# Gated linear attention before a maxout layer: sums kept in PSUM on VectorE, and all queues in a new order

## The chip, the cores and the metric

One core of one Trainium2 chip. The time is that of the device for one execution, in microseconds (us). The kernel before took 141.57 us (median of 3 runs, 141.08 to 141.87). The engines are named as in the profile: PE (TensorE), DVE (VectorE), ACT (ScalarE), POOL (GpSimd) and SP (SyncE, which here issues DMAs).

## The reference, cut to what matters

```python
batch, n_heads, seq, head_dim = (4, 8, 768, 48)      # q, k, v, f_logit, float32
f = 1.0 / (1.0 + np.exp(-f_logit))
for t in range(S):
    state = f[:, :, t, :, None] * state + np.einsum('bhd,bhe->bhde', k[:, :, t], v[:, :, t])
    y[:, :, t] = np.einsum('bhd,bhde->bhe', q[:, :, t], state)
x = y.transpose(0, 2, 1, 3).reshape(3072, 384)
out = np.maximum(x @ w1, x @ w2) @ w_out             # w1, w2: 384 x 1024, w_out: 1024 x 384
```

A linear attention whose 48 x 48 state decays by a gate of its own in each row, and behind it a layer with the greater of two products.

## The kernel before, in words

The 768 positions of each of the 4 batches are cut into 3 windows of 256, so there are 12 units of work, numbered s = 4 * window + batch (0 to 11). A partition holds an even position and the odd one behind it; the upper and the lower 64 partitions are the two halves of a window, h = 0 and 1, with one update of the state each. Within a half the positions meet through a masked product (A, m), over the halves through the state.

The greater of two products is computed as relu(x (w1 - w2)) w_out + x (w2 w_out). So the weights need work of their own at the start: the difference `wd` (in four quarters), w_out cast, w2 transposed, and the product `m2` of w2 and w_out.

Everything is cut into steps, and the text `ORDER` lists them. Each engine works through its own steps in that order, and waits where an operand is not ready or a buffer is not free. A word of it is a step's letters, its unit (and part), its engine where there is a choice (v = DVE, a = ACT, p = POOL, s = SP), and behind @ the PSUM bank that it uses (0 to 7), or for a load the slot in SBUF. Texts below name steps in this way, mostly without the bank: `Q5p` is step Q of unit 5 on POOL. The steps, with the line that the profile shows:

- loads on SP: `Lf Lk Lq Lv` (inputs, L114), `Wa Wb` (halves of w1 and w2, L125), `Wo` (halves of w_out, L129); stores `O` (L439) and `P` (parts of the last unit, L433)
- ACT: `E` (L191), `F` (L195), `G` (L199) make the gate's logarithm and its exponentials from f; `X` (`inv`, L216) and `Z` (`dec`, L221) are exponentials of the sums that `C` left in PSUM
- DVE or POOL: `e` (L202) adds the logarithms of a pair; `i` (L225) and `K` (L236) scale k; `j` (L229, DVE) and `Q` (L239) scale q; `V` (L103) casts v. Their inputs lie in SBUF
- PE: `C` (L206, L209) cumulative sums; `t`, `u` (L256) transpose K's and Q's results into a pair of banks; `A` (L273) products of q and k, two parts; `S` (L313) starts the output with the state's part, `y` (L341) finishes it; `D` (L357) sums k and v for the new state
- out of PSUM: `U` (L103, `trs`) copies t's and u's result; `m` (L281, DVE) masks A's; `z` (L329, DVE) reads one column, so that `y` comes behind `S`; `Y` (L103, `xT`) copies the output of `y`
- the state, part h: `n` (L373, DVE) adds D's sum and the state before, `N` (L378, DVE or POOL) multiplies by the decay in `dec`; where there is no state before, `n` (L375) multiplies the sum by the decay at once, and no N follows
- the layer: PE `d` (L396, four parts of a unit, 6 matmuls each) multiplies by `wd`, `r` (L405 on ACT, L407 on DVE) applies relu to two parts, PE `o` (L417 with `m2`, 3 matmuls; L420, 8 matmuls) gives the output, `b` (L103, `ob`) copies it
- weights: `wc` casts w2 (L103), PE `wt` (L456) transposes it, `wx` copies that out of PSUM, `wo` casts w_out, PE `wm` (L472) forms `m2`, `wn` copies it, `ws` (L482) forms a quarter of `wd`

The result of `n` lies in SBUF (`tmp_s`, float32, three buffers), whoever does the N behind it. The bank of `D` can be written again when `n` has read it.

Of the kernel before, what the change touches and what calls it, by code (L numbers as in the profile page):

```python
# [17 lines left out]


ORDER = """  # L20
Lf0s@12 Lk0s@13 Lq0s@14 Lv0s@15 E0 Lf1s@16 F0 Lk1s@17 e0v G0 i0v C0@0 Lq1s@12 Z0 X0 K0v V0a Lv1s@18
j0v D0@0 Q0v t0@2 Wb0s E1 n0.0v u0@2 n0.1v F1 Wa0s U0v@2 N0.1p Wb1s G1 Wa1s e1v A0.0@2 Wo0s i1p C1@0
Wo1s m0.0v@2 A0.1@4 X1 S0@6 Z1 K1p m0.1v@4 Lf2s@16 V1a z0 y0 j1v t1@4 Q1v Y0a@6 wc0a u1@4 D1@0 U1v@4
wc1a wt0@6 ws0p n1.0v A1.0@4 A1.1@2 n1.1v m1.0v@4 S1@0 wt1@7 ws1p Lf3s@12 wx0v@6 d0.0@4 z1 wx1a@7
m1.1v@2 wc3p d0.1@5 wc2a wt3@7 ws2v y1 r0.0a@4 wt2@6 ws3v Y1a@0 d0.2@4 Lq2s@0 wo1p wx2v@6 d1.2@0
wx3a@7 d1.0@2 wo0p Lk2s@2 d1.1@3 wo3a wo2p d0.3@5 r1.0v@2 Lv2s@10 wm0@7 E2 r0.1v@4 F2 Lq3s@16 wm2@6
E3 e2p wn0v@7 wm1@4 Lk3s@11 F3 j2v wn2a@6 e3p C2@7 wn1v@4 d1.3@1 Lv3s@12 G2 X2 i2v o0.0@6 Z2 K2v
Lf5s@8 V2a Q2v t2@4 r1.1a@0 D2@2 Lf4s@10 u2@4 n2.0v C3@7 j3v G3 o1.0@0 Lq4s@0 N1.1p X3 U2v@4 b0.0a@6
i3p Z3 n2.1v A2.0@4 Lk4s@2 K3p S2@6 A2.1@2 m2.0v@4 o0.1@1 V3a b1.0a@0 Lv4s@12 m2.1v@2 Q3p E5 D3@4 z2
t3@2 F5 Lk5s@11 b0.1v@1 y2 n3.0v N2.1p E4 u3@2 n3.1v e5p o1.1@1 Y2v@6 Lv5s@16 F4 U3v@2 G4 e4p  # L30
Lq5s@10 d2.0@6 b1.1a@1 j4v C4@0 A3.0@2 i4p X4 A3.1@4 Lf7s@8 d2.1@7 m3.0v@2 Z4 K4p G5 d2.2@0 r2.0a@6
Lf8s@9 m3.1v@4 S3@2 d2.3@1 V4a Q4p C5@6 z3 r2.1v@0 y3 Lq7s@3 X5 t4@4 Y3a@2 D4@0 O0s u4@4 n4.0v Z5
d3.0@2 Lq6s@0 i5v U4a@4 d3.2@6 j5v Lf6s@12 d3.1@3 K5v d3.3@7 r3.0a@2 N4.0p Lk7s@11 o2.0@4 Q5p n4.1v
E7 r3.1v@6 F7 t5@2 V5v A4.0@6 Lk6s@10 A4.1@0 b2.0a@4 e7p u5@2 m4.0v@6 o2.1@5 U5a@2 N3.1p Lv6s@16
m4.1v@0 C7@4 S4@6 b2.1a@5 j7v A5.0@0 Lv7s@8 D5@2 X7 N4.1p z4 o3.0@5 n5.0v Z7 N5.0v E6 Q7p Lq8s@2
n5.1v m5.0v@0 E8 S5@2 y4 b3.0a@5 Lv10s@9 j6v A5.1@0 F6 o3.1@5 m5.1v@0 Y4a@6 e6p O2s Lf9s@3 z5 G6
d4.0@6 G7 b3.1v@5 i6p O1s C6@4 d4.2@0 X6 i7v y5 Z6 K6v Lq11s@12 d4.1@7 Y5a@2 K7v Lk8s@10 d4.3@1
r4.0a@6 Q6v d5.0@2 Lf11s@11 t6@4 r4.1a@0 N5.1p t7@6 u6@4 V7p u7@6 d5.1@3 U6v@4 F8 d5.2@0 r5.0a@2
U7v@6 D7@4 Lf10s@8 d5.3@1 V6a o4.0@2 n7.0v r5.1a@0 N7.0p Lk9s@0 e8v G8 j8v A7.0@6 Lq9s@16 D6@0 n7.1v
C8@3 n6.0v o4.1@4 Z8 m7.0v@6 N6.0p Lq10s@6 X8 Q8p b4.0a@2 n6.1v A7.1@6 b4.1a@4 S7@0 O3s A6.0@2  # L40
m7.1v@6 o5.0@5 E9 Lv8s@7 i8p F9 z7 Lk10s@3 m6.0v@2 G9 e9p y7 V10a Lv9s@2 A6.1@2 N7.1p S6@6 o5.1@4
b5.0a@5 m6.1v@2 E10 z6 F10 Y7v@0 C9@2 O4s y6 X9 Lk11s@8 j9v b5.1a@4 d7.0@0 K8v Z9 O5s d7.2@4 E11 Q9p
Y6v@6 d7.1@1 F11 Lv11s@11 d6.0@6 r7.0a@0 d7.3@5 i9v d6.1@7 K9v r7.1a@4 d6.2@2 V8v t9@0 r6.0a@6 e11v
t8@4 u9@0 u8@4 d6.3@3 U9v@0 U8a@4 o7.0@6 r6.1v@2 A8.1@4 j11v b7.0a@6 A9.0@0 A8.0@2 V9p D8@7 G10
o7.1@6 m8.0v@2 G11 i11p n8.0v m8.1v@4 o6.1@7 N8.0p b7.1a@6 i10p O7s m9.0v@0 N6.1p C11@4 D9@5 X11
A9.1@0 S8@2 n9.0v o6.0@6 Z11 z8 N9.0p m9.1v@0 Q11p S9@0 y8 z9 e10v y9 b6.0v@6 Y8a@2 C10@4 b6.1v@7
Y9a@0 d8.0@2 K11v O6s d8.2@6 Z10 X10 d9.0@0 K10v d9.2@4 d9.1@1 j10v d8.1@3 Q10p r9.0a@0 d9.3@5
r8.0v@2 d8.3@7 r9.1a@4 t10@0 r8.1v@6 t11@2 u10@0 u11@2 o9.0@4 U10a@0 U11v@2 V11v A11.0@2 b9.0a@4
A10.0@0 A11.1@6 m11.0v@2 D11@5 o8.1@4 m11.1v@6 o8.0@2 n11.0v m10.0v@0 N11.0p S11@6 b8.0a@2 D10@5
A10.1@0 z11 n10.0v y11 N10.0v m10.1v@0 S10@2 o9.1@5 Y11a@6 b8.1a@4 z10 y10 b9.1v@5 O9s d11.0@4  # L50
Y10v@2 O8s d11.2@0 d11.1@5 d11.3@1 r11.0a@4 d10.0@2 d10.2@6 r11.1v@0 d10.1@3 d10.3@7 r10.0a@2
o11.0@0 r10.1a@6 o10.0@1 b11.0v@0 P11.0s o10.1@0 b10.0v@1 o11.1@6 b10.1v@0 O10s o11.2@7 b11.1v@6
P11.1s b11.2a@7 P11.2s
"""


# [1 line left out]
def kernel(  # L58
# [311 lines left out]
    def step_n(s, h):  # L370
        if has_state(s, h):
            tmps[s, h] = work.tile([C, NP, D], F32, name="tmp_s", tag="tmp_s", bufs=3)
            nc.vector.tensor_add(tmps[s, h], sadd[s][h][:, :, 0:D], state_before(s, h)[:, 1::2, :])  # L373
        else:
            nc.vector.tensor_mul(state_of(s)[:, h, 1::2, :], sadd[s][h][:, :, 0:D], decay(s, h))  # L375

# [167 lines left out]
```

## Time and profile before

The profile shows one execution. Its first line gives the span, from the first instruction to the last.

| | |
|---|---|
| time of the profiled execution | 141.12 us |
| its span | 139.3 us |
| median of 3 runs | 141.57 us |
| instructions in the span | 5772 |
| mean granted clock of PE | 1.000 |
| DMA: bytes and mean rate over the span | 28.68 MB, 206 GB/s |

The engines' lines of the page give busy us, the share of the span, and behind x the instructions. The line of digits gives the busy share in tenths in 40 equal slices of the span, 3.48 us each. A group of instructions shows the engine, the operation, output <- inputs, their sizes, the count, then busy us, the mean ns of one, and behind a bar the idle time just before them with what ended it. A row of the timeline begins with its start and duration in us. A row of the waits gives the total us, how many times, and the longest.

### The profile page before, as it was taken

The numbers are of one execution on the slowest core, as the hardware profiler recorded it, in microseconds if no ns is written. First come the engines' busy times: TensorE is split into PE (matmuls) and PEld (weight loads), VectorE is DVE, ScalarE is ACT, GpSimd is POOL, SyncE is SP. The second block draws the span as 40 slices with busy tenths as digits, with TensorE's granted clock in tenths as the row PEclk, the third lists the DMA queues.
The fourth block names the chain that finished last, engine by engine and source line by source line (L and its number), as shares of the span: only waits on it lengthen the run. The fifth ranks groups of instructions, "written<-read, shape, count | busy, mean of one in ns | idle before, by whom it ended". The sixth has DMA issues, their size and how long they took to land.

```text
span 139.3 us, 5772 instructions
## 1 busy us (share of the span) xinstructions
PE 122.4 (88%) x2575; PEld 91.6 (66%) x2575; DVE 99.6 (72%) x155; ACT 83.1 (60%) x119; POOL 56.6 (41%) x64
## 2 busy tenths in 40 slices
PE   0026699999899999996999999999999999999991
PEld 0024677876567788665688657886678876778670
DVE  5778968756988787789778686967957689643130
ACT  3646464769677679796578687978126470404400
POOL 7604519526188795736601382530860501000000
PEclk9999999999999999999999999999999999999999
DMA  4999999999999999999999999891113000032014
GB/s 112 271 261 264 374 386 378 334 257 238 274 266 239 256 268 274 273 263 253 292 316 273 244 260 292 239 319 50 59 59 118 0 5 7 5 132 98 3 53 169
DMA packets 54617, 28.68 MB, mean 206 GB/s; under 512 B 50240, under 2 KB 51648, under 8 KB 54592
## 3 DMA queue, kind: packets, MB, share of 16 engines
q1 hardware_dynamic: 54592, 28.32, 76.7%
q8 instruction: 20, 0.33, 1.0%
q14 instruction: 5, 0.04, 0.1%
HBM read 23.59 MB, written 4.72 MB: 203 GB/s over the span
## 4 chain that ended last, share of the span: by engine, by line
PE 79%; DMA 9%; DVE 3%; POOL 3%; SPq 2%; ACT 2%; issue 1%; DVEq 0%; POOLq 0%
PE banks L396 23%; PE banks L420 21%; PE banks L417 9%; DMA slots<-in_moe_w_dram 6%; PE banks L341 5%; PE banks L256 4%; PE banks L273 4%; PE banks L313 4%; PE banks L472 3%; DMA slots<-in_f_logit_dram 3%; POOL wd L482 3%; PE banks L357 2%; PE banks L206 2%; DVE st L378 1%; SPq L114 1%; SPq L125 1%
## 5 line engine op out<-in xcount | busy, mean ns | idle before, releaser
L420 PE MATMUL banks<-wo,gT 128*128 128x384 bf16 (+2 forms) x200 | 35.3, 320 | 0.0
L396 PE MATMUL banks<-xT,wd 128*128 128x256 bf16 x288 | 34.6, 274 | 0.3 <-POOL wd L482 0.3
L281 DVE TENSOR_TENSOR at_m<-banks,mask 128x1024 bf16<-128x1024 f32 x24 | 28.7, 1218 | 6.0 <-PE banks L273 6.0
L396 PEld LDWEIGHTS <-wd 128*128 128x128 bf16 x288 | 27.3, 98 | 4.5 <-POOL wd L482 0.6
L420 PEld LDWEIGHTS <-gT 128*128 128x128 bf16 x200 | 19.3, 98 | 12.0
L405 ACT ACTIVATE gT<-banks 128x1024 bf16<-128x1024 f32 x16 | 16.0, 1022 | 9.5 <-PE banks L396 9.2
L239 POOL TENSOR_TENSOR qp<-slots,dec 128x768 bf16<-128x768 f32 x8 | 15.1, 1888 | 11.4 <-ACT dec L221 6.0
L103 ACT COPY ob<-banks 128x384 f32<-128x384 f32 (+2 forms) x18 | 9.0, 501 | 16.8 <-PE banks L420 14.1
L378 POOL TENSOR_TENSOR st<-tmp_s,dec 128x192 bf16<-128x192 f32 x14 | 7.9, 566 | 23.6 <-DVE tmp_s L373 21.4
L417 PE MATMUL banks<-m,xT 128*128 128x384 bf16 (+2 forms) x75 | 16.1, 321 | 0.4 <-DVE m L103 0.4
L407 DVE TENSOR_SCALAR gT<-banks 128x1024 bf16<-128x1024 f32 x8 | 9.7, 1222 | 5.7 <-PE banks L396 5.3
L191 ACT ACTIVATE gate<-slots 128x768 f32<-128x768 f32 x12 | 10.0, 845 | 4.6 <-DMA slots<-in_f_logit_dram 4.6
L103 DVE COPY ob<-banks 128x384 f32<-128x384 f32 (+2 forms) x11 | 5.9, 542 | 8.5 <-PE banks L420 8.1
L103 DVE COPY trs<-banks 128x2048 bf16<-128x2048 bf16 x8 | 9.7, 1220 | 3.0 <-PE banks L256 3.0
L341 PE MATMUL banks<-at_m,vb 64*64 64x128 bf16 x576 | 11.7, 224 | 0.0
L103 ACT CAST xT<-banks 128x768 bf16<-128x768 f32 x8 | 6.4, 798 | 8.8 <-PE banks L341 8.7
L225 POOL TENSOR_TENSOR slots<-slots,one 128x384 f32<-128x384 f32 x7 | 7.6, 1084 | 9.8 <-ACT one L199 6.4
L273 PE MATMUL banks<-trs 48*64 48x128 bf16 x384 | 9.6, 234 | 1.3 <-DVE trs L103 1.3
L313 PE MATMUL banks<-trs,st 48*64 48x128 bf16 x240 | 8.7, 227 | 2.2 <-DVE look L329 1.1
L195 ACT ACTIVATE ell<-gate 128x768 f32<-128x768 f32 x12 | 10.1, 843 | 0.6
L236 DVE TENSOR_TENSOR kp<-slots,inv 128x768 bf16<-128x768 f32 x9 | 8.6, 963 | 2.6 <-issue 1.4
L206 PE MATMUL banks<-e,u_inc 128*128 128x384 bf16 x12 | 4.3, 356 | 6.8 <-DVE e L202 6.8
(64 smaller groups left out, 180.1 us busy)
## 6 DMA issues: line engine op xcount, KB each, us to landing
slots<-in_f_logit_dram SPq DMA_DIRECT2D x12, 384.0 KB, 6.3
slots<-in_k_dram SPq DMA_DIRECT2D x12, 384.0 KB, 6.4
slots<-in_q_dram SPq DMA_DIRECT2D x12, 384.0 KB, 6.2
slots<-in_v_dram SPq DMA_DIRECT2D x12, 384.0 KB, 6.1
out_dram<-ob SPq DMA_DIRECT2D x11, 384.0 KB, 5.4
slots<-in_moe_w_dram SPq DMA_DIRECT2D x4, 768.0 KB, 9.1
...
```

Source lines behind the costliest of these rows:

```text
L103: (nc.scalar.copy if e == "a" else engines[e].tensor_copy)(out, in_)
L191: nc.scalar.activation(flat(gate[s]), flat(loaded[s]["f"]), AF.Exp, bias=0.0, scale=-1.0)
L195: nc.scalar.activation(flat(ell[s]), flat(gate[s]), AF.Ln, bias=1.0, scale=1.0)
L239: engines[e].tensor_mul(pad("qp", s)[:, :, :, 0:D], by_parity(loaded[s]["q"]), both(dec[s][:, 0:HD].rearrange("p (h d) -> p h d", h=H)))
L273: nc.tensor.matmul(out=ps[h * HC:(h + 1) * HC, j % 2, par, :], lhsT=t[rows, h, 0, j, par, :], rhs=t[rows, h, 1, j].rearrange("p a t -> p ( ...
L281: nc.vector.tensor_mul(at[s][:, jj].rearrange("p r j a t -> p (r j) (a t)"), banks[:, b:b + 2, :].rearrange("p r (j x) -> p (r j) x", j=2) ...
L313: nc.tensor.matmul(out=ys[s][h][cols, kt, :], lhsT=window(state_before(s, h)[rows], head // 2, off), rhs=tr[s][rows, h, 1, head // 2].rear ...
L341: nc.tensor.matmul(out=ys[s][h][cols, kt, :], lhsT=window(vb[rows, par], head, off), rhs=m[rows, head // 4, head % 2, head // 2 % 2, par, ...
L396: nc.tensor.matmul(out=ps[:, f, :], lhsT=wd[:, kt, ff * C:(ff + 1) * C], rhs=x_flat(g)[:, kt, :], start=(kt == 0), stop=(kt == KT - 1))
L405: nc.scalar.activation(dst, src, AF.Relu)
L417: nc.tensor.matmul(out=ps, lhsT=x_flat(g)[:, kt, cols], rhs=m2[:, kt, m], start=(kt == 0), stop=False)
L420: nc.tensor.matmul(out=ps, lhsT=gT[g][:, ff, cols], rhs=wo[:, ff, m], start=False, stop=(ff == FG - 1))
```

## The change

A sum whose N is done by DVE stays where D left it: `n` adds the state before to it in its PSUM bank, and N reads it there. For the other N nothing changes but the order.

```diff
+    words = ORDER.split()
...
     def step_n(s, h):
         if has_state(s, h):
-            tmps[s, h] = work.tile([C, NP, D], F32, name="tmp_s", tag="tmp_s", bufs=3)
-            nc.vector.tensor_add(tmps[s, h], sadd[s][h][:, :, 0:D], state_before(s, h)[:, 1::2, :])
+            sums = sadd[s][h][:, :, 0:D]
+            tmps[s, h] = sums if f"N{s}.{h}v" in words else work.tile([C, NP, D], F32, name="tmp_s", tag="tmp_s", bufs=3)
+            nc.vector.tensor_add(tmps[s, h], sums, state_before(s, h)[:, 1::2, :])
```

The order is new as a whole: the same 540 steps, with other places, banks and slots, and for some another engine. It was made with GpSimd and VectorE holding each other up as their steps come. The steps with a choice of engine go, before and after, to:

| step | before | after |
|---|---|---|
| e | 5 DVE, 7 POOL | 1 DVE, 11 POOL |
| i | 5 DVE, 7 POOL | 4 DVE, 8 POOL |
| K | 9 DVE, 3 POOL | 8 DVE, 4 POOL |
| Q | 4 DVE, 8 POOL | 6 DVE, 6 POOL |
| V | 7 ACT, 3 DVE, 2 POOL | 5 ACT, 2 DVE, 5 POOL |
| N | 2 DVE, 14 POOL | 6 DVE, 10 POOL |
| r | 16 ACT, 8 DVE | 20 ACT, 4 DVE |
| b | 16 ACT, 9 DVE | 18 ACT, 7 DVE |
| wc | 3 ACT, 1 POOL | 2 ACT, 1 POOL, 1 DVE |
| wn | 2 DVE, 1 ACT | 3 DVE |
| wo | 3 POOL, 1 ACT | 2 POOL, 2 ACT |
| U, Y, ws, wx | | the same numbers |
| P | 3 SP | 2 SP, 1 ACT |

The start of the order, up to the first `o`:

```
before:
Lf0s@12 Lk0s@13 Lq0s@14 Lv0s@15 E0 Lf1s@16 F0 Lk1s@17 e0v G0 i0v C0@0 Lq1s@12 Z0 X0 K0v V0a Lv1s@18
j0v D0@0 Q0v t0@2 Wb0s E1 n0.0v u0@2 n0.1v F1 Wa0s U0v@2 N0.1p Wb1s G1 Wa1s e1v A0.0@2 Wo0s i1p C1@0
Wo1s m0.0v@2 A0.1@4 X1 S0@6 Z1 K1p m0.1v@4 Lf2s@16 V1a z0 y0 j1v t1@4 Q1v Y0a@6 wc0a u1@4 D1@0 U1v@4
wc1a wt0@6 ws0p n1.0v A1.0@4 A1.1@2 n1.1v m1.0v@4 S1@0 wt1@7 ws1p Lf3s@12 wx0v@6 d0.0@4 z1 wx1a@7
m1.1v@2 wc3p d0.1@5 wc2a wt3@7 ws2v y1 r0.0a@4 wt2@6 ws3v Y1a@0 d0.2@4 Lq2s@0 wo1p wx2v@6 d1.2@0
wx3a@7 d1.0@2 wo0p Lk2s@2 d1.1@3 wo3a wo2p d0.3@5 r1.0v@2 Lv2s@10 wm0@7 E2 r0.1v@4 F2 Lq3s@16 wm2@6
E3 e2p wn0v@7 wm1@4 Lk3s@11 F3 j2v wn2a@6 e3p C2@7 wn1v@4 d1.3@1 Lv3s@12 G2 X2 i2v o0.0@6 Z2 K2v
...
after:
Lf0s@12 Lk0s@13 Lq0s@14 Lv0s@15 E0 Lf1s@16 F0 Lk1s@12 G0 e0p i0v C0@0 Lq1s@17 j0v X0 Z0 K0v Lv1s@18
V0a Q0p D0@0 Wb0s t0@2 n0.0v E1 n0.1v u0@2 F1 Wa0s U0v@2 Wb1s G1 e1p Wa1s N0.1v S0@2 Wo0s A0.0@0 i1p
Wo1s z0 C1@4 m0.0v@0 A0.1@6 X1 Z1 Lf2s@16 K1p j1v V1a Q1v m0.1v@6 t1@4 wc0a u1@4 D1@0 U1a@4 y0 n1.0v
n1.1v wt0@6 ws0p N1.1v ws1v Y0a@2 A1.0@4 S1@0 m1.0v@4 wx0a@6 A1.1@2 Lf3s@12 wc2p wc3a d0.0@6 z1
m1.1v@2 wt2@4 d0.1@7 ws2v ws3p y1 r0.0a@6 wc1v d0.2@2 Y1a@0 wt1@5 d0.3@3 wo1a Lq2s@17 wx1v@5 wo0p
d1.0@0 r0.1v@2 wx2a@4 wt3@5 Lk2s@18 d1.1@1 wx3v@5 wo3a wo2p d1.2@2 r1.0v@0 wm0@5 Lv2s@0 E2 wm1@4 F2
wn0v@5 Lk3s@16 E3 e2p wm2@5 wn1v@4 Lq3s@10 F3 j2v C2@4 G2 e3p d1.3@3 wn2v@5 Lf4s@12 Z2 o0.1@5 i2v X2
Q2p G3 K2v Lf5s@11 r1.1a@2 C3@4 V2v t2@0 X3 u2@0 Lv3s@0 D2@2 U2a@0 o1.0@6 i3p n2.0v n2.1v Lk4s@17
...
```

Around the update of the state in unit 5, and at the end:

```
before:
m4.1v@0 C7@4 S4@6 b2.1a@5 j7v A5.0@0 Lv7s@8 D5@2 X7 N4.1p z4 o3.0@5 n5.0v Z7 N5.0v E6 Q7p Lq8s@2
n5.1v m5.0v@0 E8 S5@2 y4 b3.0a@5 Lv10s@9 j6v A5.1@0 F6 o3.1@5 m5.1v@0 Y4a@6 e6p O2s Lf9s@3 z5 G6
...
o11.0@0 r10.1a@6 o10.0@1 b11.0v@0 P11.0s o10.1@0 b10.0v@1 o11.1@6 b10.1v@0 O10s o11.2@7 b11.1v@6
P11.1s b11.2a@7 P11.2s
after:
C6@1 Lf8s@12 d3.3@3 b2.1v@0 X6 S4@6 Z6 D5@4 z4 r3.1a@2 A5.0@0 Lv7s@8 n5.0v y4 N5.0p F7 o3.0@2 n5.1v
j7v Lk9s@11 Y4a@6 e7p m5.0v@0 G7 d4.0@6 N5.1p O2s b3.0v@2 Lv6s@9 C7@3 i6p A5.1@4 j6v X7 S5@0 o3.1@2
...
d10.3@3 r10.0a@0 d11.2@4 d11.0@6 r10.1a@2 d11.3@5 d11.1@7 o10.1@2 r11.0v@6 r11.1v@4 o10.0@3 o11.0@4
b10.0a@3 b10.1v@2 O10s o11.1@5 b11.0a@4 P11.0a o11.2@4 b11.1a@5 P11.1s b11.2a@4 P11.2s
```

More of the change, by code (lines that the diff above doesn't have):

```diff
@@ L20 @@
 ORDER = """
[L21 to L53, printed above, removed]
+Lf0s@12 Lk0s@13 Lq0s@14 Lv0s@15 E0 Lf1s@16 F0 Lk1s@12 G0 e0p i0v C0@0 Lq1s@17 j0v X0 Z0 K0v Lv1s@18
+V0a Q0p D0@0 Wb0s t0@2 n0.0v E1 n0.1v u0@2 F1 Wa0s U0v@2 Wb1s G1 e1p Wa1s N0.1v S0@2 Wo0s A0.0@0 i1p
@@ new lines @@
+Q2p G3 K2v Lf5s@11 r1.1a@2 C3@4 V2v t2@0 X3 u2@0 Lv3s@0 D2@2 U2a@0 o1.0@6 i3p n2.0v n2.1v Lk4s@17
+N2.1v K3p j3v Z3 A2.0@0 A2.1@2 b1.0a@6 o0.0@4 m2.0v@0 Lq4s@18 E4 Q3v F4 Lv4s@12 t3@0 S2@6 m2.1v@2
+b0.0a@4 u3@0 e4p E5 o1.1@4 Lk5s@10 U3v@0 V3p F5 Lq5s@11 b0.1a@5 z2 A3.0@0 e5p y2 b1.1a@4 m3.0v@0 G4
+A3.1@4 C5@2 Lf6s@0 Y2a@6 i4p C4@3 m3.1v@4 D3@0 Z4 d2.0@6 X4 Lk6s@16 n3.0v d2.2@4 X5 n3.1v d2.1@7 Z5
+K4v N3.1p Lv5s@8 G5 S3@2 V4p d2.3@5 r2.0a@6 z3 j4v t4@0 i5p Q4v y3 Lf7s@12 r2.1a@4 D4@6 K5p u4@0
+Y3v@2 o2.0@4 Lk7s@18 U4a@0 n4.0v j5v N4.0v O1s Q5p d3.0@2 n4.1v Lq7s@10 b2.0a@4 N4.1v A4.0@0 E6
@@ new lines @@
+A4.1@4 t5@6 m4.0v@0 Lq6s@17 d3.1@3 F6 V5p u5@6 m4.1v@4 G6 o2.1@0 Lf9s@0 r3.0a@2 e6v E7 U5v@6 d3.2@2
+C6@1 Lf8s@12 d3.3@3 b2.1v@0 X6 S4@6 Z6 D5@4 z4 r3.1a@2 A5.0@0 Lv7s@8 n5.0v y4 N5.0p F7 o3.0@2 n5.1v
+j7v Lk9s@11 Y4a@6 e7p m5.0v@0 G7 d4.0@6 N5.1p O2s b3.0v@2 Lv6s@9 C7@3 i6p A5.1@4 j6v X7 S5@0 o3.1@2
+Z7 z5 Q6p Lq9s@2 m5.1v@4 E9 F9 K6v O0s d4.1@7 Q7p d4.2@4 b3.1a@2 i7v Lq8s@16 r4.0a@6 y5 K7v t6@2 G9
+Lf10s@18 t7@6 Y5a@0 u6@2 e9p u7@6 d4.3@5 U6v@2 Lv9s@10 d5.0@0 r4.1a@4 U7v@6 C9@2 d5.1@1 X9 d5.2@4
@@ new lines @@
+V7v Z9 A7.0@6 r5.0a@0 Lk8s@8 D7@2 d5.3@5 n7.0v N7.0v o4.0@0 r5.1a@4 n7.1v Lq10s@17 m7.0v@6 N7.1p V6a
+A7.1@2 Lk11s@0 i9v A6.0@6 b4.0a@0 D6@4 m7.1v@2 o4.1@1 E8 Lf11s@9 F8 m6.0v@6 o5.1@2 G8 Lv11s@12 n6.0v
+b4.1v@1 N6.0p e8p j9v A6.1@0 Lv8s@3 S7@6 E10 o5.0@3 m6.1v@0 i8p O3s z7 n6.1v Lk10s@18 S6@0 N6.1p
+b5.0a@3 y7 z6 Q9p j8v b5.1a@2 Lv10s@6 y6 j10v Y7a@6 C8@2 Y6v@0 V9a d7.0@6 O4s d7.2@4 X8 Lq11s@10 Z8
+d7.1@7 F10 Q8v d6.0@2 d7.3@5 r7.0a@6 e10p K9v d6.1@3 V8p r7.1a@4 K8v d6.2@6 t9@0 r6.0a@2 t8@4 u9@0
@@ new lines @@
+u8@4 d6.3@7 U9v@0 E11 o7.0@2 G10 U8v@4 r6.1a@6 i10p A9.1@0 b7.0a@2 D8@3 D9@6 A9.0@4 F11 n8.0v o7.1@7
+N8.0p m9.0v@4 V11a n9.0v o6.0@4 N9.0p b7.1v@7 e11p m9.1v@0 V10p C10@5 S9@6 X10 A8.1@0 A8.0@2 z9 j11v
+y9 Z10 b6.0v@4 o6.1@5 Y9a@6 m8.0v@2 G11 Q10v i11p d9.0@2 b6.1a@5 C11@4 m8.1v@0 O6s d9.1@3 Z11 O7s
+d9.2@6 O5s X11 r9.0a@2 K11p S8@4 d9.3@7 z8 K10v y8 r9.1a@6 Q11v D10@2 t11@0 Y8a@4 t10@6 n10.0v u11@0
+u10@6 N10.0p d8.0@4 U11v@0 U10a@6 d8.2@2 d8.1@5 A11.0@0 r8.0a@4 A10.0@6 d8.3@3 m10.0v@6 o9.0@4
@@ L54 @@
+r8.1a@2 m11.0v@0 D11@5 b9.0a@4 A10.1@0 S10@2 A11.1@6 o8.0@4 m11.1v@6 n11.0v o9.1@6 m10.1v@0 N11.0p
+z10 S11@0 b9.1a@6 y10 z11 b8.0a@4 O9s y11 Y10v@2 o8.1@4 Y11v@0 d10.0@0 b8.1v@4 d10.2@2 O8s d10.1@1
+d10.3@3 r10.0a@0 d11.2@4 d11.0@6 r10.1a@2 d11.3@5 d11.1@7 o10.1@2 r11.0v@6 r11.1v@4 o10.0@3 o11.0@4
+b10.0a@3 b10.1v@2 O10s o11.1@5 b11.0a@4 P11.0a o11.2@4 b11.1a@5 P11.1s b11.2a@4 P11.2s
 """
@@ L510 @@
     }
-    for word in ORDER.split():
+    for word in words:
         key, of, e, b = re.fullmatch(r"([A-Za-z]+)([0-9.]+)([avps]?)@?([0-9]*)", word).groups()
```

## The prediction

> **What bounds the kernel now.** I read the page's first two parts, then the table of stages of 4 us, then the waits of TensorE (PE), then the timelines of VectorE (DVE) and GpSimd (POOL).
>
> ```profile
> PE 122.4 (88%) x2575; PEld 91.6 (66%) x2575; DVE 99.6 (72%) x155; ACT 83.1 (60%) x119; POOL 56.6 (41%) x64
> PE   0026699999899999996999999999999999999991
> ```
>
> PE is the engine to watch, and its idle time has three places. The table of stages gives PE 4.28 busy us in the first 16, so 11.7 idle; the last instruction of PE ends at 136.24 of 139.3, so 3.06 idle after it; 139.3 - 122.4 = 16.9 leaves 2.1 between 16 and 136. Half of that is one gap:
>
> ```profile
> 60.00:64.00 4.00, 3.59 (x81) 2.26 (x78) 3.40 (x5) 3.80 (x7) 1.81 (x1) 1.00 1.16 262
> 64.00:68.00 4.00, 3.36 (x100) 2.58 (x101) 3.42 (x6) 2.48 (x5) 1.76 (x2) 1.00 1.04 254
> ```
>
> ```profile
> PE banks L313 <- DVE tmp_s L373: 1.0, 1, 1.0
> ```
>
> The first number after the stage's 4.00 is PE's: 0.41 and 0.64 idle us. The wait says that S5 (L313) stood behind an `n`. The timelines tell why that `n` was late:
>
> ```profile
> 62.07 1.81 POOL L239 TENSOR_TENSOR qp<-slots,dec 128x768 bf16<-128x768 f32 x1 [2.23 <-ACT dec L221]
> 62.23 1.87 DVE L378 TENSOR_TENSOR st<-tmp_s,dec 128x192 bf16<-128x192 f32 x1
> 120.07 0.36 DVE L378 TENSOR_TENSOR st<-tmp_s,dec 128x192 bf16<-128x192 f32 x1
> ```
>
> The same N takes 0.36 us alone and 1.87 us when GpSimd began Q5 0.16 us before it: it ended 0.22 us after Q5 did (63.88 and 64.10). DVE's operations with two inputs in SBUF do this: seen for N, j, i and ws, and I take e, K and Q, of the same kind, with them. j takes 0.55 us alone and up to 1.33, i 0.55 and 1.58 beside a Q. One that comes late ends about 0.41 us (0.55 kind), 0.82 us (0.96 kind, from ws beside a GpSimd cast: 1.10) after GpSimd's. It works the other way too: GpSimd's i took 1.38 instead of 1.00 beside a j. PSUM inputs do not do it: `n` and `m` run their 0.35 and 1.22 us beside busy GpSimd. I call this a hold. DVE lost some 4.7 us to holds (seven: N 1.5, i 1.0, j 0.8, 0.5, 0.3, 0.3 and 0.2; and a little of ws), but PE only the 1.05 above.
>
> From 35.35 on PE is full but for that gap, so the rest of the run is 136.24 - 35.35 = 100.9 us, 99.85 of it work. The time can change in two ways only: PE comes to that point (call it T0, the first `o`) at another time, or it loses other time behind it.
>
> **What the new order leaves alone.** PE has the same 176 steps. A step of the full array (d, o, C, wt) behind one of part of it costs some 0.1 us more (three matmuls of L417 take 0.59 in the chain and 0.49 behind another `o`); there are 28 such changes in either order, so PE's work is equal. The first 14 loads are the same, in the same order; Lk1 now waits for E0's slot, which E0 has read at 5.26, and was issued at 5.74 anyway. Moves between engines, by rows: DVE gives 4 r (1.22), 4 e (0.55), 2 b, K, V, i and takes 2 Q (0.95), 4 N (0.35), wc, wn: some -6 us. ACT takes 4 r (1.02) and 2 b, gives 2 V (0.83): +3. POOL takes 4 e (1.00), a K (1.81), 3 V (about 0.85), an i and gives 2 Q and 4 N: +4. None comes near PE; only order matters.
>
> **The sums in PSUM.** Six N now read the sum from PSUM, and the dec beside it is the only SBUF input, so no hold.
>
> ```profile
> L375 DVE TENSOR_TENSOR st<-banks,dec 128x192 bf16<-128x192 f32 x4 | 1.4, 350 | 0.2 <-PE banks L357 0.2
> L373 DVE TENSOR_TENSOR tmp_s<-banks,st 128x192 f32<-128x192 f32 x16 | 5.6, 353 | 3.6 <-PE banks L357 3.0
> ```
>
> L375 is the new N's form: 0.35 us. [...] No row has a DVE operation that writes PSUM, as these `n` now do; I bound it by 0.26 (DVE's memset of 240 elements, L164, which reads nothing) and 0.70 (twice the row), and take 0.35, its own form but for the place. Either way six of them are 2 us at most of a DVE that is idle 40 us. The bank is held 0.35 us longer; the next PE step on it is over 2 us of PE work away wherever I looked.
>
> **The start, step by step** (times of the span; before in brackets). e0 goes to POOL: 6.17 to 7.17 (6.73). C0, 0.58, then X0 0.48: 8.25 (8.26, because X now precedes Z). K0 stays at 8.3 to 9.3, j0 having moved ahead of it, and D0 still waits for V0, whose load ends at 8.95. Q0 on POOL waits for K0 and ends at 11.0 (10.71); u0, U0: 12.95 (12.71). S0 and A0.0 stand before C1: m0.0 begins at 13.9 (13.45), X1 14.35 (13.96), K1 ends 16.7 (16.40). j1 is held by K1, 17.1; Q1 18.1 (17.88). m0.1 now stands behind j1 and Q1 and ends at 19.25 (15.81). So y0, which PE did at 15.92, comes behind t1, u1 (18.15) and D1 (to 19.2) and runs to 20.95, at the slow pace that PE shows there (48 matmuls of L341 in 1.7 us; 0.67 later). wt0, A1.0, S1, A1.1: 22.9, d0.0 to 23.9 (22.5 to 23.6).
>
> ```profile
> 20.27 3.58 POOL L482 TENSOR_TENSOR wd<-slots 128x768 bf16<-128x768 f32 x2 [3.88 <-DMA slots<-in_moe_w_dram]
> 24.32 1.97 DVE L482 TENSOR_TENSOR wd<-slots 128x768 bf16<-128x768 f32 x2 [0.22 <-DMA slots<-in_moe_w_dram]
> ```
>
> These show when the weight halves are in: 20.2 and 24.3. ws0 on POOL is 20.27 to 22.08; ws1, now on DVE behind N1.1 (20.4), is held: 22.9. m1.0, queued behind it, ends at 24.05, m1.1 at 25.3. ws2 meets ws3 (POOL, 24.3 to 26.1) and ends at 26.9. d0.2 needs it: **27.0 (26.5)**. From there PE has d0.2, wt1, d0.3, d1.0, wt3, d1.1, d1.2, three wm, C2, d1.3: six d 4.05, two wt 0.95, wm 3.9, C2 0.25, together 9.15, to 36.15, with no wait that I find. Before had its last wt done by 26.5, ended d1.3 at 34.77 and then waited 0.58 for the last m2 copy, which the new order covers with d1.3. **T0: 36.15 against 35.35, +0.80.** Bounds: -0.2 (ws2 has the port before ws3, d0.2 at 26.0) and +1.8 (PE's slow pace lasts through y1 and d0.2, another 1.0).
>
> **Behind T0.** The 1.05 gap goes: N5.0 and N5.1 are on POOL, DVE has nothing between n5.0 and n5.1 that can be held, and o3.0, d4.0, C7 and A5.1 (3.0 us) stand on PE between D5 and S5. What is late next: C2 now ends at 35.45, Z2 at 36.0, so Q2 (POOL) holds the port 36.0 to 37.8 and K2 (DVE), ready at 36.4, ends at 38.6. PE has o0.1 and C3 until 38.2: +0.45. In the same way j4 behind V4 puts Q4 at 53.6, u4 waits 0.15. Walking on to o2.0 I find no more. For the 80 us that I did not walk I take +0.5, half of what the old order lost behind T0. I also set, by these rows, the queued work of an engine against PE's work between what releases it and the step that needs it: under 0.35 us is left in 6 places of the old order and in 11 of the new. Bounds 0 and 2.0 (three holds of the mean size, 4.7/7 = 0.67).
>
> **The end.** d10 and d11 (8 times 0.66) and five o are as before. P11.0 is issued by ACT, ahead of b11.1 and b11.2. No row has ACT issuing; SP's issues take 0.33 to 1.44. At 0.33 the 1.83 us of o11.1 and o11.2 cover it: 0, which I take (the nearest row is the same P at 0.33); at 1.44 it costs 0.45.
>
> **Sum:** +0.80 - 1.05 + 0.45 + 0.15 + 0.5 = **+0.85 us**. The profiled execution took 141.12 us (139.3 of span, 1.8 around it), 0.45 under the median of the runs: 141.97 by the first, and **142.4** by the median, 141.57 + 0.85.
>
> **Rivals.**
> Forecast, late start and new holds (0.42): 141.9 to 143.2.
> Not slower, DVE has the port first (0.24): ws1 and ws0 are both ready within 0.15 us of 20.3. If DVE begins ws1 before POOL begins ws0, ws1 ends at 21.3 instead of 22.9; m1.0 then waits for A1.0 alone, and m1.1 ends at 24.45, or at 24.0 if PE is past its slow pace. It decides at 24.3, when the second half of w1 lands: with m1.1 done by then ws2 begins there, ahead of ws3, d0.2 is at 25.4, T0 at 34.55, 1.6 before the forecast's, and the sum is +0.85 - 1.6 = -0.75: 140.8, and 140.3 where the 0.5 of the unwalked part does not come either. For it: the DVE queue before ws1 is short. Against: by my walk POOL is 0.1 us earlier.
> Same (0.18): the late start and the gap's gain cancel, +0.80 - 1.05 = -0.25, and the holds behind T0 (0.60 and 0.5) are covered by half: +0.3, 141.9 at most.
> Much slower (0.16): the 11 tight places meet holds, since POOL has more operations of 1.00 and 1.81. Walked terms +0.35, three holds +2.0: 143.9; with an ACT issue of 1.44, +0.45: 144.4.
> The sums in PSUM alone do nothing (inside all of these): N as slow as 1.87 would show a hold in spite of PSUM.
>
> A measurement here tells 0.5% (0.7 us) from no change. Faster by more: the second, 0.24. Within: the third, and 0.09 of the forecast's, 0.27. Slower: 0.33 + 0.16 = 0.49. Range: 140.2 to 144.0, from the fast rival to the slow one without the dear issue.
>
> **What would show it.** Right: y0 at 19 to 21; ws1 and ws2 of nearly 2 us; d0.2 at 27, the first `o` at 36; N on DVE 0.35 beside a busy POOL; K2 of about 2.2 us with PE idle before t2. Wrong: a first `o` before 35.4, or over 1.5 us of PE idle behind it.

## The result and the profile after

The changed kernel takes 146.66 us (median of 4 runs, 146.13 to 147.51), beside 141.32 us for the kernel before (median of 4, 140.90 to 141.87): a ratio of 1.038, with a 95% interval of 1.032 to 1.045. The prediction said 142.4 us, 140.2 to 144.0; it had the sign and not the size. The profiled execution took 146.51 us, with a span of 144.7. The ratios below leave disturbed executions out, so a median can stand above what its ratio gives.

First the engines' lines of the page of the changed kernel.

```profile
PE 122.7 (85%) x2575; PEld 91.2 (63%) x2575; DVE 104.0 (72%) x150; ACT 85.6 (59%) x122; POOL 64.1 (44%) x66
...
PE   0046399799799998997959999999999899999991
```

PE's busy time has hardly moved (122.4 before), so its idle time has grown from 16.9 to 22.0 us; the digits of 7 and the 5 in mid-run are new. DVE should have become 6 us lighter and is 4.4 heavier (99.6 before), though it has 5 instructions less. The table of stages (columns as before: PE, its weight loads, DVE, ACT and POOL busy, then clock and DMA) shows where PE stands still:

```profile
36.00:40.00 4.00, 2.75 (x49) 1.76 (x47) 3.86 (x3) 2.68 (x5) 3.91 (x3) 1.00 1.17 260
...
60.00:64.00 4.00, 4.00 (x72) 2.85 (x72) 3.17 (x4) 2.96 (x6) 0.02 (x1) 1.00 1.21 277
64.00:68.00 4.00, 3.28 (x123) 2.32 (x114) 2.47 (x5) 2.76 (x4) 2.79 (x4) 1.00 1.16 263
...
72.00:76.00 4.00, 2.27 (x96) 1.80 (x95) 3.66 (x3) 2.27 (x4) 2.95 (x2) 1.00 0.76 219
```

The old gap at S5 in 60 to 64 is gone, as predicted. In its place PE is idle 1.25 us in 36 to 40 and 1.73 in 72 to 76. In both stages DVE and POOL are busy nearly throughout. What PE waited for (of the second row 0.2 us, and of the others nothing, lies still in the start):

```profile
PE banks L256 <- DVE kp L236: 2.6, 3, 1.7
...
PE banks L256 <- DVE qp L239: 0.8, 2, 0.5
...
PE banks L418 <- issue: 0.7, 1, 0.7
PE banks L357 <- DVE vb L103: 0.6, 1, 0.6
PE banks L357 <- DVE kp L236: 0.4, 1, 0.4
```

All but the third row wait for results of DVE steps whose operands lie in SBUF: K, Q and V. The timeline of DVE and POOL shows two of them, K2 with V2 and K7:

```profile
36.35 2.36 DVE L236 TENSOR_TENSOR kp<-slots,inv 128x768 bf16<-128x768 f32 x1
38.63 1.35 DVE L103 CAST vb<-slots 128x768 bf16<-128x768 f32 x1
...
70.85 1.16 DVE L236 TENSOR_TENSOR kp<-slots,inv 128x768 bf16<-128x768 f32 x1
71.93 2.17 DVE L225 TENSOR_TENSOR slots<-slots,one 128x384 f32<-128x384 f32 x1
74.20 1.56 DVE L236 TENSOR_TENSOR kp<-slots,inv 128x768 bf16<-128x768 f32 x1
...
36.01 1.88 POOL L239 TENSOR_TENSOR qp<-slots,dec 128x768 bf16<-128x768 f32 x1 [1.61 <-ACT dec L221]
37.86 1.71 POOL L225 TENSOR_TENSOR slots<-slots,one 128x384 f32<-128x384 f32 x1
...
69.37 4.31 POOL L239 TENSOR_TENSOR qp<-slots,dec 128x768 bf16<-128x768 f32 x2 [0.90 <-DVE slots L229]
73.65 1.31 POOL L202 TENSOR_TENSOR e<-ell 128x384 bf16<-128x384 f32 x1
```

Around 36 us K2 (0.96 alone) comes 0.34 us behind Q2 and takes 2.36; the cast V2 (0.55 alone) then meets `i3` and takes 1.35. Around 70 us Q6 and Q7 follow each other on POOL, 4.31 us together. Between them K6 takes 1.16, `i7` (0.55 alone) 2.17, and K7, beside e9, 1.56. The two engines pass the hold to and fro: POOL's own steps lengthen too (`i3` 1.71 instead of 1.00). In PE's rows this becomes 0.66 us ahead of t2, 0.63 ahead of D2 and 1.73 ahead of t7:

```profile
38.77 0.41 PE L256 MATMUL banks<-ident,kp 64*128 64x64 bf16 x16 [0.66 <-DVE kp L236]
...
40.04 0.44 PE L357 MATMUL banks<-vb,kp 64*64 64x48 bf16 x32 [0.63 <-DVE vb L103]
...
75.83 0.41 PE L256 MATMUL banks<-ident,kp 64*128 64x64 bf16 x16 [1.73 <-DVE kp L236]
```

The groups of DVE show which steps were held, and that the new N were not. The first two rows are of the kernel before, the others of the changed one:

```profile
L236 DVE TENSOR_TENSOR kp<-slots,inv 128x768 bf16<-128x768 f32 x9 | 8.6, 963 | 2.6 <-issue 1.4
L225 DVE TENSOR_TENSOR slots<-slots,one 128x384 f32<-128x384 f32 x5 | 3.8, 757 | 0.0
...
L236 DVE TENSOR_TENSOR kp<-slots,inv 128x768 bf16<-128x768 f32 x8 | 12.0, 1514 | 0.5 <-ACT inv L216 0.3
L239 DVE TENSOR_TENSOR qp<-slots,dec 128x768 bf16<-128x768 f32 x6 | 7.8, 1301 | 0.1
L225 DVE TENSOR_TENSOR slots<-slots,one 128x384 f32<-128x384 f32 x4 | 4.2, 1044 | 1.4 <-ACT one L199 1.4
...
L379 DVE TENSOR_TENSOR st<-banks,dec 128x192 bf16<-128x192 f32 x6 | 2.1, 353 | 0.1
```

K has a mean of 1.51 us where it had 0.96, its time alone; i has 1.04 where it had 0.76 and takes 0.55 alone. Summed over all DVE instructions, the time above the duration alone is 14.2 us, against 4.8 in the kernel before (K 4.5, i and j 4.4, Q 2.1, ws 2.1, casts 1.2, N none); on POOL it is 7.3 against 2.8. I call these sums the holds of a kernel.

### The profile page after: what moved, and what is told of

It is laid out like the page before. It is cut to its first block, busy times and chain, and to the rows that moved or that the text cites. A ratio compares the mean times of both kernels' runs of the same rounds, so it can differ in the third digit from the quotient of the medians.

```text
span 144.7 us, 5784 instructions
## 1 busy us (share of the span) xinstructions
PE 122.7 (85%) x2575; PEld 91.2 (63%) x2575; DVE 104.0 (72%) x150; ACT 85.6 (59%) x122; POOL 64.1 (44%) x66
## 4 chain that ended last, share of the span: by engine, by line
PE 65%; DVE 19%; issue 6%; ACT 3%; DMA 3%; POOL 2%; DVEq 0%
PE banks L421 20%; PE banks L397 16%; PE banks L418 8%; DVE kp L236 7%; PE banks L273 4%; PE banks L256 4%; DVE qp L239 3%; PE banks L313 3%; PE banks L473 3%; DMA slots<-in_f_logit_dram 3%; DVE wd L483 2%; PE banks L357 2%; PE banks L341 2%; POOL qp L239 2%; DVE slots L225 1%
## 5 line engine op out<-in xcount | busy, mean ns | idle before, releaser
L406 ACT ACTIVATE gT<-banks 128x1024 bf16<-128x1024 f32 x20 | 20.3, 1024 | 13.4 <-PE banks L397 13.3
L421 PEld LDWEIGHTS <-gT 128*128 128x128 bf16 x200 | 19.3, 98 | 12.9 <-issue 1.0
L103 ACT COPY ob<-banks 128x384 f32<-128x384 f32 (+3 forms) x20 | 9.7, 494 | 16.9 <-PE banks L421 16.9
L379 POOL TENSOR_TENSOR st<-tmp_s,dec 128x192 bf16<-128x192 f32 x10 | 5.7, 574 | 30.6 <-DVE tmp_s L374 30.6
L202 POOL TENSOR_TENSOR e<-ell 128x384 bf16<-128x384 f32 x11 | 12.2, 1108 | 11.0 <-ACT ell L195 11.0
L239 POOL TENSOR_TENSOR qp<-slots,dec 128x768 bf16<-128x768 f32 x6 | 12.0, 2010 | 4.6 <-ACT dec L221 3.2
L236 DVE TENSOR_TENSOR kp<-slots,inv 128x768 bf16<-128x768 f32 x8 | 12.0, 1514 | 0.5 <-ACT inv L216 0.3
L225 POOL TENSOR_TENSOR slots<-slots,one 128x384 f32<-128x384 f32 x8 | 9.4, 1171 | 5.8 <-ACT one L199 5.8
L216 ACT ACTIVATE inv<-banks 128x384 f32<-128x384 f32 x12 | 5.8, 489 | 10.0 <-PE banks L209 10.0
L341 PEld LDWEIGHTS <-vb 64*64 64x64 bf16 x576 | 10.1, 111 | 0.2 <-issue 0.2
L103 ACT COPY trs<-banks 128x2048 bf16<-128x2048 bf16 x4 | 7.5, 1866 | 4.4 <-PE banks L256 4.4
```

What stands on the lines that cost most here:

```text
L103: (nc.scalar.copy if e == "a" else engines[e].tensor_copy)(out, in_)
L202: engines[e].tensor_add(pad("e", s)[:, :, 0:D], ell[s][:, :, 0, :], ell[s][:, :, 1, :])
L225: engines[e].tensor_mul(even, even, one[s])
L236: engines[e].tensor_mul(pad("kp", s)[:, :, :, 0:D], by_parity(loaded[s]["k"]), both(inv[s]))
L239: engines[e].tensor_mul(pad("qp", s)[:, :, :, 0:D], by_parity(loaded[s]["q"]), both(dec[s][:, 0:HD].rearrange("p (h d) -> p h d", h=H)))
L341: nc.tensor.matmul(out=ys[s][h][cols, kt, :], lhsT=window(vb[rows, par], head, off), rhs=m[rows, head // 4, head % 2, head // 2 % 2, par, ...
```

## The experiments

**Theory:** the 3.8% is holds between DVE and POOL, in the places where the new order puts DVE's K, Q, i, j and V beside longer POOL steps. **Rivals:** the sums in PSUM cost the time; the moves of steps between engines do, whatever the order; the order of PE, SP and the banks does, with the holds as mere company.

Four numbers are compared for most kernels: the start of the first `o`; from there to the end of PE's last instruction PE's busy and idle time; and DVE's holds. "Before" began its first `o` at 34.59 and stood 0.43 us inside it, which is why the prediction counted 35.35.

| kernel | ratio | first `o` | PE busy behind it | PE idle behind it | DVE held |
|---|---|---|---|---|---|
| before | 1 | 34.59 | 100.2 | 1.5 | 4.8 |
| after | 1.038 | 35.91 | 100.9 | 5.0 | 14.2 |
| e2: before, sums in PSUM | 0.991 | 34.85 | 100.3 | 0.9 | |
| e5: after, POOL only writes | 1.000 | 34.72 | 100.0 | 1.1 | 0.9 |
| e6: before, POOL only writes | 0.994 | 35.34 | 99.8 | 0.0 | 0.0 |
| e7: after, Q7 moved | 1.031 | 35.95 | 101.1 | 3.5 | |
| e10: after, three steps moved | 1.020 | 36.05 | 100.6 | 2.4 | 11.4 |

**e1: the new order, its sums back in SBUF.**

```diff
-            tmps[s, h] = sums if f"N{s}.{h}v" in words else work.tile([C, NP, D], F32, name="tmp_s", tag="tmp_s", bufs=3)
+            tmps[s, h] = work.tile([C, NP, D], F32, name="tmp_s", tag="tmp_s", bufs=3)
```

> The changed kernel with every sum of n in SBUF again, as before; order and engines stay. Theory 'holds' (the loss behind the first o comes from VectorE and GpSimd holding each other at the SBUF port): the sums in PSUM play no part in the loss, so 146 to 147.5 us, and the six N on VectorE, which now have two inputs in SBUF, show a hold or two (over 0.5 us instead of 0.36). Rival 'sums' (n and N in the PSUM bank cost time themselves or keep the bank too long): it falls by 1 us or more, to 145 or under.

Measured: 148.64 us, 1.046 (1.039 to 1.053). The group of N on DVE is held again:

```profile
L379 DVE TENSOR_TENSOR st<-tmp_s,dec 128x192 bf16<-128x192 f32 x6 | 3.4, 574 | 0.1
```

574 ns a piece against 353, and no time is won: the rival "the sums cost it" is dead. The time lies above what was expected (146 to 147.5). How much the sums save here stays open. The intervals of e1 and of the change overlap, and part of e1's time is another thing: its wait ahead of t7 is 2.28 us instead of 1.73, and behind it the granted clock fell (last section). Of e1's four executions three have a mean clock of 0.988 to 0.989 and take 148.4 us or more; the one with 1.000 took 147.14, inside the changed kernel's 146.13 to 147.51.

**e2: the old order, with the new `n` alone** (`words = ORDER.split()` and the changed lines of `step_n`, in the kernel before).

> The kernel before, with its own order, and only the new n: the two sums whose N is on VectorE (5.0 and 10.0) stay in PSUM. Theory 'holds': N5.0 takes 0.35 us beside Q5 on GpSimd instead of 1.87, PE's gap of 1.05 us before S5 goes, and the time is 140.3 us (0.993 of before; 0.990 to 0.997). Rival: another wait takes the gap's place, or the longer hold on the bank costs as much: 141.3, ratio 0.998 to 1.002.

Measured: 140.33 us, 0.991 (0.988 to 0.994): the sums in PSUM are worth 0.9% by themselves. It is the best version of this study, though e8 is no different within the error. Its timeline where the kernel before had the gap at S5:

```profile
63.02 0.36 DVE L380 TENSOR_TENSOR st<-banks,dec 128x192 bf16<-128x192 f32 x1
...
62.86 1.81 POOL L240 TENSOR_TENSOR qp<-slots,dec 128x768 bf16<-128x768 f32 x1 [2.22 <-ACT dec L222]
```

The same N beside the same Q5, begun 0.16 us behind it as before: 0.36 us instead of 1.87, and `n5.1` is no longer late.

**e3 and e5: the new order, with GpSimd's steps replaced by ones that only write.** Each elementwise step on POOL becomes a product of one column, which keeps what it waits for, memsets of about the step's length, and in e3 a second product of one column.

```diff
+    def idle_pool(out, in0, in1, times):
+        first = tuple([slice(None)] + [slice(0, 1)] * (len(out.shape) - 1))
...
+            nc.gpsimd.tensor_tensor(out[first], in0[first], (in1 if in1 is not None else in0)[first], op=ALU.mult)
...
+        for part in times:
+            nc.gpsimd.memset(part, 0.0)
```

> The changed kernel in which each elementwise step or cast on GpSimd (e, i, K, Q, V, N, and ws, wc, wo of the weights) is left out: in its place GpSimd does a product of one column (which waits for the same inputs), memsets of the output that last about as long (two of the output, 1.0 us for e and i, 1.8 for K and Q), and one column again; so the results are not the reference's. Order, waits and the engines' times stay, but GpSimd hardly reads SBUF. Theory 'holds': VectorE's j, i, K, Q take 0.55 and 0.96 us, PE's idle time behind the first o falls from 5.0 us to 1.5 or less, and the time to 142 to 143.5 us. Rival 'order' (the new queues are late by themselves: places, banks, ACT's four more r): PE keeps 3.5 us or more of idle time there and the time is over 145. If writes by GpSimd hold VectorE just as reads do, the holds stay and the time with them.

Measured: 1.045 (1.036 to 1.053). DVE's holds fell to 0.9 us, and yet no time was won, against what was expected (142 to 143.5). The waits of PE tell why:

```profile
PE banks L282 <- POOL qp L106: 4.5, 4, 1.6
PE banks L282 <- POOL kp L106: 3.7, 3, 3.1
```

The replacements were too long. POOL was busy 78.3 us instead of 64.1, since a product of a single column mostly takes 0.2 to 0.4 us there, and PE now waited for POOL's own K and Q. Inconclusive; e5 is the same with the second product left out and the memsets cut to the steps' time alone.

> As e3 (GpSimd's elementwise steps and casts left out of the changed kernel, memsets of the outputs in their place, so the results are not the reference's), but with their length cut to that of the real steps: e3's GpSimd steps came out longer than the real ones (a product of one column alone takes 0.25 to 0.31 us), and PE then waited for GpSimd's K and Q. Now one such product ahead, and memsets: 1.0 us for e and i, 1.8 for K, Q, ws, 0.5 for N, 0.94 for casts. Theory 'holds': VectorE's j, i, K, Q stay at 0.55 and 0.96 us as in e3, PE's waits for K, Q, V behind the first o fall from 5.0 us to under 1.5, and the time is 141 to 143. Rival 'order': over 3.5 us of waits and over 145.

Measured: 141.88 us, **1.000 (0.996 to 1.004)**. The page, and the groups of DVE:

```profile
PE 120.5 (87%) x2575; PEld 90.1 (65%) x2575; DVE 91.3 (66%) x150; ACT 85.7 (62%) x122; POOL 59.0 (42%) x146
```

```profile
L255 DVE TENSOR_TENSOR kp<-slots,inv 128x768 bf16<-128x768 f32 x8 | 7.6, 955 | 0.7 <-ACT inv L230 0.4
L262 DVE TENSOR_TENSOR qp<-slots,dec 128x768 bf16<-128x768 f32 x6 | 5.7, 954 | 0.7 <-ACT dec L235 0.5
L241 DVE TENSOR_TENSOR slots<-slots,one 128x384 f32<-128x384 f32 x4 | 2.2, 552 | 1.4 <-ACT one L211 1.4
...
L115 DVE CAST vb<-slots 128x768 bf16<-128x768 f32 x2 | 1.6, 800 | 0.0
```

K, Q and i are at their times alone, DVE is 12.7 us lighter than in the changed kernel, and the 3.8% is gone, with the order, the engines and the banks left as they are. POOL is not lighter than it would be without its own holds: 59.0 us against 64.1 - 7.3 = 56.8. The profiled span is 5.6 us shorter: the first `o` comes 1.2 earlier, behind it PE is idle 3.9 us less and busy 0.9 less, and what follows PE's last instruction is 0.4 longer. At the start Q1, ws1 and ws2 are no longer held (0.96, 0.96 and 0.97 us instead of 2.38, 2.26 and 1.75). PE also left its slow pace earlier in this execution (wt0 takes 0.51 us instead of 0.82), so not all of the 1.2 need be holds.

**e6: the same replacement in the kernel before**, as a control: POOL's steps might gain by becoming cheaper rather than by holding less.

> The same replacement in the kernel before (its results are not the reference's either), as the control of e5. Theory 'holds': the kernel before lost 1.05 us behind the first o to a hold and perhaps 0.5 ahead of it, so it gains 1.0 to 1.7: 139.7 to 140.4 us, much less than e5 gains on the changed kernel (4 us). If the replacement itself makes any kernel faster (fewer waits, shorter GpSimd steps), this one gains 3 us or more too.

Measured: 140.83 us, 0.994 (0.990 to 0.998). The engines' line of its page:

```profile
PE 122.8 (89%) x2575; PEld 92.0 (67%) x2575; DVE 95.1 (69%) x155; ACT 83.0 (60%) x119; POOL 52.2 (38%) x138
```

DVE loses its 4.8 us of holds (99.6 before). The old order gains 0.6% by the replacement, a little less than expected, the new one 3.8%. So the replacement by itself makes up at most a small part of e5's gain; the rest is due to holds that are the new order's own. And the new order, freed of holds, is no better than the old one freed of them (1.000 and 0.994).

**e4 and e9: the moves against the order.** e4 is the new order with every step back on its old engine, e9 the old order with the new engines and the new `n`; in each 73 of the 540 words change their engine's letter, as here in e4's first words:

```diff
-Lf0s@12 Lk0s@13 Lq0s@14 Lv0s@15 E0 Lf1s@16 F0 Lk1s@12 G0 e0p i0v C0@0 Lq1s@17 j0v X0 Z0 K0v Lv1s@18
+Lf0s@12 Lk0s@13 Lq0s@14 Lv0s@15 E0 Lf1s@16 F0 Lk1s@12 G0 e0v i0v C0@0 Lq1s@17 j0v X0 Z0 K0v Lv1s@18
```

In e9 some sums are read from a bank that its next user has already rewritten, since the old order puts other steps on the bank between `n` and N (N1.1 is one); part of the state is thus made from other data, and its time is read for the engines and the order alone.

> The changed kernel's order, places, banks and slots, with each step on the engine that it had before (so e, K, V, i, N, Q, r, b move back). Theory 'holds' in the form 'the moves made them': with four e, three V and a K fewer on GpSimd the holds on VectorE fall from some 14 us to under 8 and the time to 143 to 144.5. Form 'the order made them' (steps placed side by side whatever their engine), or rival 'order': 146 or more, since this order was not laid out for these engines.

> The order, places, banks and slots of the kernel before, with each step on the engine that the changed kernel gives it (four e, a K, an i and three V more on GpSimd and so on) and the new n. With e4 (new order, old engines, 151.8) it completes the table of order by engines. Theory 'the moves made the holds': the longer GpSimd steps hold VectorE by 10 us or more and the time is 145 or more. Form 'each order is laid out for its own engines': 145 or more as well, with PE waiting for late GpSimd steps, not only for held ones. If the moves are harmless by themselves: 140 to 142.

Measured: e4 1.063 (1.060 to 1.066), e9 1.074 (1.068 to 1.080). With the two kernels themselves that makes a square: old order with old engines 1, with new 1.074; new order with old engines 1.063, with new 1.038. Neither half alone is the cause. Each order fits its own engines, and the crossed kernels wait in many other places, as a row of e9's PE shows:

```profile
58.66 0.24 PE L314 MATMUL banks<-trs,st 48*64 48x128 bf16 x2 [2.12 <-DVE look L330]
```

For e4, what was expected if the moves were the cause (143 to 144.5 us) failed. Its DVE is held 8.7 us in all, less than the changed kernel's, and it is slower still: the sum of the holds does not give the time, it matters who waits behind them, and here PE also waits 1.7 us for POOL's own Q. By its time e4 came out on the side of the order, but e5, which keeps the whole order, shows that the order costs nothing where nothing is held.

**e7: one held place undone.** Q7 goes from POOL to DVE, behind K7.

```diff
-Z7 z5 Q6p Lq9s@2 m5.1v@4 E9 F9 K6v O0s d4.1@7 Q7p d4.2@4 b3.1a@2 i7v Lq8s@16 r4.0a@6 y5 K7v t6@2 G9
+Z7 z5 Q6p Lq9s@2 m5.1v@4 E9 F9 K6v O0s d4.1@7 d4.2@4 b3.1a@2 i7v Lq8s@16 r4.0a@6 y5 K7v Q7v t6@2 G9
```

> The changed kernel with one step moved: Q7 goes from GpSimd, where it stands behind Q6 and ahead of e9, to VectorE, directly behind K7. In the changed kernel i7 (2.17 us) and K7 (1.56) on VectorE wait for Q7 and e9 on GpSimd, and PE waits 1.73 us for K7 before t7. Theory 'holds': i7 takes 0.55, K7 0.96 or a little more (beside e9), PE waits under 0.6 us there, and the time falls by 1.0 to 1.5 us, to 145.0 to 145.6 (ratio 1.025 to 1.031 where the changed kernel's is 1.038). Rival 'order': VectorE, with 0.95 us more to do ahead of t7 and u7, is later still, and the time stays or rises.

Measured: 145.47 us, 1.031 (1.025 to 1.037). The timeline of DVE and PE:

```profile
71.74 1.35 DVE L225 TENSOR_TENSOR slots<-slots,one 128x384 f32<-128x384 f32 x1
73.19 0.96 DVE L236 TENSOR_TENSOR kp<-slots,inv 128x768 bf16<-128x768 f32 x1
...
74.21 0.41 PE L256 MATMUL banks<-ident,kp 64*128 64x64 bf16 x16 [0.29 <-DVE kp L236]
```

`i7`, now beside e9 (1.11 us on POOL, from 71.56), takes 1.35 instead of 2.17 (0.55 was expected), K7 0.96 instead of 1.56, and t7 waits 0.29 instead of 1.73. PE's idle time behind the first `o` falls by 1.5 us, the time by 0.7%, at the upper end of what was expected. The intervals of e7 and of the change overlap, so what shows the gain is the wait in the trace, more than the time.

**e10: three.** Q7 as in e7, Q2 from POOL to DVE behind K2, and V2 from DVE to ACT.

```diff
-Q2p G3 K2v Lf5s@11 r1.1a@2 C3@4 V2v t2@0 X3 u2@0 Lv3s@0 D2@2 U2a@0 o1.0@6 i3p n2.0v n2.1v Lk4s@17
+G3 K2v Q2v Lf5s@11 r1.1a@2 C3@4 V2a t2@0 X3 u2@0 Lv3s@0 D2@2 U2a@0 o1.0@6 i3p n2.0v n2.1v Lk4s@17
```

> The changed kernel with three steps moved away from a hold: Q7 to VectorE behind K7 as in e7, Q2 from GpSimd to VectorE behind K2, and V2 from VectorE to ACT. Theory 'holds': K2 (2.36 us, beside Q2) takes 0.96 and PE's wait of 0.66 us before t2 goes; V2 (a cast, 1.35 us on VectorE beside i3 on GpSimd, 0.55 alone) no longer delays D2, and PE's 0.63 us there goes; with e7's 1.0 to 1.2 together 2.0 to 2.5 us, so 144.0 to 144.6 (ratio 1.019 to 1.024). Rival 'order': later waits take the places of these and it stays within 0.5 of e7's 145.5.

Measured: 144.62 us, 1.020 (1.015 to 1.025), at the upper end of what was expected and clear of the change's 1.032 to 1.045. K2's row on DVE is now

```profile
36.48 0.96 DVE L236 TENSOR_TENSOR kp<-slots,inv 128x768 bf16<-128x768 f32 x1
37.35 0.95 DVE L239 TENSOR_TENSOR qp<-slots,dec 128x768 bf16<-128x768 f32 x1
```

and the waits ahead of t2 and D2 are gone. Three words give back about half of the loss. The rest lies in the late start (the first `o` at 36.05, 34.72 in e5) and in smaller waits.

**e8: an attempt to beat e2.** In e2 the first `o` still stands 0.3 us inside, behind wn1, a copy of `m2`, which DVE does behind j2. j2 is put behind it.

```diff
-E3 e2p wn0v@7 wm1@4 Lk3s@11 F3 j2v wn2a@6 e3p C2@7 wn1v@4 d1.3@1 Lv3s@12 G2 X2 i2v o0.0@6 Z2 K2v
+E3 e2p wn0v@7 wm1@4 Lk3s@11 F3 wn2a@6 e3p C2@7 wn1v@4 j2v d1.3@1 Lv3s@12 G2 X2 i2v o0.0@6 Z2 K2v
```

> The kernel before with its own order, the new n (sums in PSUM for N5.0 and N10.0 on VectorE, as e2), and one step moved: j2 goes from ahead of wn1 to behind it on VectorE. In the kernel before, j2 is held by e3 on GpSimd (1.33 us instead of 0.55), and wn1 behind it makes PE wait 0.43 us in o0.0. Theory 'holds': that wait goes and nothing takes its place, so 0.4 to 0.6 us less than e2's 140.33: 139.8 (ratio 0.986 to 0.989). Rival: j2, now later, makes Q2 and u2 late: as e2 or up to 0.5 slower than it.

Measured: 140.35 us, 0.993 (0.990 to 0.996): a miss. The wait went, but the later j2 now met N1.1 on POOL:

```profile
34.61 0.92 DVE L230 SCALAR_TENSOR_TENSOR slots<-gate,slots 128x384 f32<-128x384 f32 x1
```

It took 0.92 us instead of 0.55, K2 came later, and PE waited 0.31 us ahead of t2. A wait was exchanged for a hold of the same size.

## Why the prediction was wrong

- **The start: right.** The first `o` was to come at 36.15 and came at 35.91, +0.56 instead of +0.80 by the prediction's count. That count sets the first matmul of `o` in the new order beside the second in the old (35.35), with 0.33 us of PE's work between them; on like terms, without the wait of 0.43, the start came 0.9 later (35.91 against 34.59 + 0.43). y0 ran from 19.26 to 20.99 (19.3 to 20.95 predicted), ws1 took 2.26 us and ws2 1.75, d0.2 began at 26.93 (27.0). One part was luck: j1 ran ahead of K1 and was not held, K1 ended at 17.40 instead of 16.7, and Q1 was held in j1's place; it ended at 18.22 where 18.1 was forecast. POOL had ws0 ahead of ws1, so the rival "DVE has the port first" did not happen; but it had the right price: with Q1, ws1 and ws2 not held the first `o` comes at 34.72 in e5 (34.55 in the rival). The port in the prediction and in e1's expectation is a name for the hold: the traces show how much longer a step takes beside one of the other engine (K2 2.36 us beside Q2, 0.96 alone), not through what.
- **The gap at S5: right**, it went. That N is not held when its sum lies in PSUM was right too (e2: 0.36 us for 1.87; 353 ns in the mean for the changed kernel's six). The rival that the sums alone do nothing is answered by e2 as well: in the old order they give 0.9%.
- **K2 and Q4: right mechanism, too small.** K2 took 2.36 us (2.2), and t2 waited 0.66 (0.45). u4 waited 0.54 (0.15).
- **Casts: missed.** The prediction let casts run free, since they have one input. V2 took 1.35 instead of 0.55, and D2 waited 0.63, in the part that the prediction had walked.
- **The failed step: "+0.5 for the 80 us that I did not walk", with bounds 0 and 2.0 from three holds of mean size.** PE's idle time behind the first `o` was 5.0 us. Of it 1.8 lie in the walked part: t2's and u4's waits (1.2 together) and D2's. The other 3.2 us, where 0.5 was put down, are t7's wait (1.73), a stall of PE without any wait at the third matmul of o3.0 (0.72, last section) and smaller ones (0.38 and 0.26 the largest). The mean of 0.67 us came from an order with seven holds on DVE, most of which fell where nobody waited; here the holds came in chains (Q6, Q7 and e9 beside K6, i7 and K7), each pushing the next into a new meeting.
- **"Some -6 us" for DVE**, by rows alone, was wrong for the same reason: it became +4.4. Without the holds it is -5.0 (99.6 - 4.8 before, 104.0 - 14.2 after), so the moves were priced well, but not what the moved steps would meet.
- **PE's own work** was to be equal and is 0.7 us longer behind the first `o` (100.9 and 100.2). This goes with the number of waits. PE is busy 99.8 us in e6, where no wait is listed there, 100.0 and 100.2 in e5 and before with two, 100.6 in e10 with five, 100.9 in the changed kernel with seven and 101.1 in e7 with eight: some 0.16 us a wait. It fits how busy time is counted: t2 takes 0.41 us to its end, but u2 begins 0.24 us behind t2's start, so the last 0.17 us of a step count only where nothing follows at once. This is a reading of the traces; no run tests it.
- **ACT's issue of P11.0** took 0.37 us (SP's reach 3.92 us in the trace before, at 20.52, not 1.44) and cost nothing: from PE's last instruction to the end it is 2.94 us (3.06 before).
- "Much slower" was the rival that came true, in kind, at a chance of 0.16, and beyond its own 144.4.

Put together, the profiled span grew by 5.4 us where the prediction had 0.85: the first `o` 1.3 later, 3.5 more idle and 0.7 more busy behind it, and 0.1 less at the end.

What the runs show as the cause: taking away the holds between DVE and POOL, and nothing of order, engines or banks, takes away the 3.8% (e5, with e6 as its control); undoing single ones gives back the time of the waits behind them (e10, and by its trace e7). What stays open is why an order made with these holds in mind ran into more of them: what lengths and arrivals it was made with is not seen in the trace.
